# Row numbers of a group's tokens made in pairs, and other orders of scatters and loads, in a convolution with a routed MoE

## The chip, the cores and the metric

One core of one Trainium2 chip runs the kernel. The metric is the device time of one execution in microseconds (us); less is better.

## The reference

A causal convolution of 7 taps over 8 sequences of 2880 tokens with 192 channels; its taps are the softmax of a given tensor, one set per token and head (8 heads of 24 channels). Each convolved token then goes to the best of 4 groups, and in it to the best of 4 experts, and through that expert's two layers (192 to 1024, relu, 1024 to 192). The output row is scaled by both softmax values.

```python
w = softmax(weight_gen)                           # 8 x 2880 x 8 heads x 7
x = einsum('bshk,bskhg->bshg', w, x_unfolded)     # 23040 tokens x 192
g = argmax(x @ w_group); e = argmax(x @ w_expert[g])
h = relu(x @ w1[g, e]);  y = h @ w2[g, e]
out[token] = softmax(group logits)[g] * softmax(expert logits)[e] * y
```

## The kernel before

The 23040 tokens are 180 columns of 128. They are taken in 16 groups: group 0 has 12 columns, group 1 has 6, groups 2 to 14 have 12 each, group 15 has 6. For each group the kernel does three things. The convolution (`conv`) is some 26 products and sums on DVE (L318, L338), 1152 elements per partition each. `route` computes logits on TensorE, picks group and expert, and works out for every token the number of its row in a DRAM buffer, `rows`, that is sorted by expert; these numbers are the tile `pos`, and L559 turns the group's whole tile into integers, `posi`. `scatters` then sends the group's tokens there: one indirect DMA per column of 128 tokens (L593, in `scatter_row`), issued on POOL. `table` (L618 to L674) works out which blocks of `rows` a round may take.

The experts' work goes in 14 rounds. Round 1 follows group 3, round r from 2 to 12 follows group r + 2, round 13 follows group 15. A round of 2 to 12 has six blocks of 256 rows of one expert each, round 13 has 13 of these and 7 of 128 rows. For a block, SP loads its rows (`xb`, L865) and the expert's weights (L882 to L889) by table entries; ACT copies part of the rows (`xd`, L948), TensorE transposes them, ACT and DVE split them in two parts (`xh`, `xlo`; DVE rounds the weights at L920 too). Then come four units of a first matmul into `ph` (L988, ten instructions), a relu on ACT (L994), and a second matmul into `py` (L1015, eight instructions). At the end of a block ACT scales each 128 rows (L1024), and POOL sends them out by an indirect DMA (L1032): two outs per block.

Each engine runs its own instructions in the order in which the program writes them. That order comes out of a planner in the kernel: `front` is a generator that writes the convolution, routing and scatters step by step, and the block loop lets it go on until clocks modelled for each engine have caught up (`fill`, `run`). A `yield` of a number is a point on the modelled clock, `NEXT` a wait for the next unit. Scatters of a group that is not routed in a hurry wait in the list `spread`, and `front` moves its first entry on once per convolution step; groups 4 to 7 yield after every second scatter, later groups after each (L578 to L585). In the kernel before only the writing is spread: the twelve scatters of a group all wait for the one `posi`. What blocks need from SP is asked for in a list (`ask`), and `pump` issues the entries; `ask_x` asks for the rows of the next block. `load_group` loads the next group's x and taps at given convolution steps (L755).

Of the kernel before, what the change touches and what calls it, by code (L numbers as in the profile page):

```python
# [8 lines left out]
F32 = mybir.dt.float32  # L9
F32R = mybir.dt.float32r  # L10
BF16 = mybir.dt.bfloat16
I32 = mybir.dt.int32
# [22 lines left out]
def conv_moe_kernel(ctx: ExitStack, tc: tile.TileContext, x, wgen, w_group, w_expert, w1, w2, out):  # L35
# [164 lines left out]
    new_raw = [ring(f"raw{i}", m, [P, n]) for i, (n, m) in enumerate(((F, 2), (F, 2), (NFT * D, 1)))]  # L200

    grp = {}
    state = {"slots": False, "open": False, "unit": 0, "starve": False, "ph": 0, "junk": None, "urgent": False}

    def ph_tile(k, shape):
        return ps_h.tile(shape, F32, name=f"ph{k}")
# [9 lines left out]
    def run(eng, cost, *deps):  # L216
        clk[eng] = max([clk[eng]] + [d + HOP for d in deps]) + cost
        return clk[eng]
# [22 lines left out]
    def round_of(g):  # L241
        return next(r for r in range(NR) if g < ENDS[r])
# [151 lines left out]
    def route(g, o):  # L394
# [157 lines left out]
        yield 0.4  # L552
        nc.vector.tensor_tensor(out=rk, in0=rk, in1=ohf, op=ALU.mult)
        yield 0.3
        ps = rt.tile([P, SG], F32, name="pos")[:, 0:n]
        nc.vector.tensor_reduce(out=ps.unsqueeze(2), in_=rk, axis=AX.X, op=ALU.add)
        yield 0.3
        pi = rt.tile([P, SG], I32, name="posi", bufs=2)[:, 0:n]
        nc.vector.scalar_tensor_tensor(out=pi, in0=ps, scalar=-1.0, in1=ps, op0=ALU.mult, op1=ALU.max)  # L559
        yield TINY  # L560
        rest = scatters(g, xrow, pi)
        if g < MAIN:
            while spread:
                for c in spread.pop(0)[0]:
                    pass
        if 0 < g < MAIN or g + 1 == ENDS[-1]:
            for i, c in enumerate(rest):
                if g >= MAIN and i % 3 == 2:
                    yield c
            if g + 1 in ENDS:  # L570
                yield from table(round_of(g))
            state["urgent"] = False
            return
# [1 line left out]
            yield from table(round_of(g), False)  # L575
        spread.append([rest, None])

    def scatters(g, xrow, pi):  # L578
        for s in range(SIZES[g]):
            run("pool", 1.28, clk["dve"])  # L580
            scatter_row(pi[:, s:s + 1], xrow[s // SC][:, s % SC, :], round_of(g))
            if not 4 <= g < 8 or s % 2:
                yield NEXT
        if g >= MAIN and g + 1 in ENDS[:-1]:
            arrive_all(round_of(g))  # L585

# [156 lines left out]
    def front():  # L743
        side, routes = [], []
        load_group(0)
        set_up()
        load_group(1)
        yield from softmax0()
        lows.append([remainders(), 0.0])
        lower_part()  # L750
        for g in range(ENDS[-1]):
            o = grp[g]
            routes.append([route(g, o), None])
            state["urgent"] = g == FIRST
            loads = [] if g in (0, ENDS[-1] - 1) else [(0 if g < FIRST + 2 else 2, 0), (8, 1)]  # L755
            ahead = 12 if g > FIRST else 4

            def soft():
                if not o.ahead and g + 1 < ENDS[-1]:
                    o.ahead = True  # L760
                    side.append([softmax(g + 1), None])

            for n, c in enumerate(conv(g, o)):
                yield c
                if loads and n >= loads[0][0]:
                    load_group(g + 1, loads.pop(0)[1])
                if n >= ahead:
                    soft()
                for q in list(soft0):
                    yield from move(soft0, q, 1)  # L770
                if not state["urgent"]:
                    for q in side[:1]:
                        yield from move(side, q, 3)
                for q in spread[:1]:
                    yield from move(spread, q, 1)
                if routes:
                    yield from move(routes, routes[0], HURRY if FIRST <= g < MAIN else 3 if g < FIRST else 8 if g in ENDS else 2)
            while loads:
                load_group(g + 1, loads.pop(0)[1])
            soft()  # L780
            yield from finish_all(side)
            yield from finish_all(routes, 1)
            yield from finish_all(spread, 1)
        yield from finish_all(spread)
        yield from finish_all(routes)

    def finish_all(qs, keep=0):
        while len(qs) > keep:
# [59 lines left out]
    def load(n, part):  # L848
        r, nb, q = order[n]
        tab = tabs[r, nb]  # L850
        if n not in visits:
            o = visits[n] = Slot()
            o.wa = None
            if not plain(n):
                i = sum(not plain(m) for m in range(n))
                o.raw = [f(i) for f in new_raw]
            o.whole = whole(n)
            o.wc, o.ev = [], None
            o.tw, o.tlo = 0.0, 0.0
        o = visits[n]  # L860
        if part == 0:
            o.xb = xbs[n % len(xbs)][:, 0:nb, :]
            o.tx = arrive[r, nb]
            rv = nc.sync.value_load(tab[q:q + 1, 0:1], min_val=0, max_val=NROW)
            ld = nc.sync.dma_start(  # L865
                out=o.xb.rearrange("p t c -> p (t c)"),
                in_=rows[bass.ds(rv, nb * UB), :].rearrange("(p t) c -> p (t c)", t=nb))
            for m in range(r + 1, NR):
                tc.declare_no_dep(ld.ins, group=f"disp{m}", reason="a later round writes later rows")
            tc.add_to_no_dep_group(f"load{r}", ld.ins)  # L870
            return
        if not plain(n):
            while lows:
                clk["pe"] = max(clk["pe"], lows[0][1])
                lower_part()
        if o.ev is None:
            o.ev = nc.sync.value_load(tab[q:q + 1, 1:2], min_val=0, max_val=NE - 1)
        if plain(n) and part < 3:
            c = slice((part - 1) * DC, part * DC)
            nc.sync.dma_start(out=new_wa(o, F32)[0:DC, part - 1, :], in_=w1v[bass.ds(o.ev, 1), c, :].rearrange("o p f -> p (o f)"))  # L880
        elif part == 1:
            nc.sync.dma_start(out=o.raw[0], in_=w1v[bass.ds(o.ev, 1), 0:P, :].rearrange("o p f -> p (o f)"))  # L882
        elif part == 2:
            for h, src in enumerate((w1v[bass.ds(o.ev, 1), P:D, :], w1lo[bass.ds(o.ev, 1), :, :])):
                nc.sync.dma_start(out=o.raw[1][h * HP:(h + 1) * HP, :], in_=src.rearrange("o p f -> p (o f)"))
        else:
            if o.whole:
                o.wc = [wp.tile([P, NFT, D], F32, name="wc", bufs=4)]
            nc.sync.dma_start(  # L889
                out=o.wc[0] if o.whole else o.raw[2].rearrange("p (f d) -> p f d", d=D),  # L890
                in_=w2v[bass.ds(o.ev, 1), :, :].rearrange("o (f p) d -> p (o f) d", p=P))
# [165 lines left out]
    def blocks(n0, n1, paced):  # L1057
        want, jobs = [], []

        def pump(upto=None):  # L1060
            for a in list(want):
# [2 lines left out]
                if upto is not None and a[0] <= upto:  # L1064
                    need(a[0])
                if not ready(a[0]) or a not in want:
                    if upto is None:
                        break
                    continue
                want.remove(a)  # L1070
                load(*a)
# [7 lines left out]

        def ask_x(n):  # L1080
            ask(n + 1, 0)
            if n < n1 and (whole(n) or n == n0 or whole(n - 1)):
                ask(n, 3)

# [152 lines left out]
```

## Time and profile before

| | |
|---|---|
| median of the runs shown | 1311.89 us |
| runs shown | 1311.4, 1311.89, 4088.56 us |
| the profiled execution | 1310.11 us |
| its span, first to last instruction | 1308.5 us |
| mean granted TensorE clock in it | 0.963 of full |
| TensorE busy | 1187.0 us, 91% |
| DVE, ACT, POOL busy | 922.6, 662.8, 439.2 us |

The profile is of one execution; the time outside its span is 1.6 us. A busy share is a mean over stages: from the start to some 55 us the first groups are prepared, to about 1016 us convolution, routing and scatters go beside the experts' blocks, and behind 1056 us only blocks are left. An engine counts as busy while an instruction executes; issuing a DMA counts on POOL, the transfer does not.

### The profile page before, as it was taken

Reading aid. Unit: us, or ns where it says so; the run is one execution under the profiler, and the core shown is the slowest. Engines: PE = TensorE matmul, PEld = TensorE weight load, DVE = VectorE, ACT = ScalarE, POOL = GpSimd, SP = SyncE. Lnnn points to the kernel's source line nnn. Section 1 sums busy time; section 2 is a strip of 40 time slices with the busy share of each in tenths; the row PEclk is TensorE's granted clock in tenths of the full one; section 3 lists DMA queues with packets and bytes.
Section 4 is the critical chain, followed back from the end, with each engine's and each line's share of the span. In section 5 each row is a group of like instructions: output and inputs, shape, how many; then the busy total and the mean of one; then the engine's idle time right before and its main releaser. Section 6 shows DMA issues by size and latency. Waiting matters only on the chain.

```text
span 1308.5 us, 25776 instructions
## 1 busy us (share of the span) xinstructions
PE 1187.0 (91%) x9047; PEld 1142.8 (87%) x9047; DVE 922.6 (71%) x1608; ACT 662.8 (51%) x1253; POOL 439.2 (34%) x411
## 2 busy tenths in 40 slices
PE   5988889899897989898989799898899899999995
PEld 5678889889797979797989799898799899999995
DVE  7867779879687878788878698787412667767600
ACT  2523236455464545454545365454445567777631
POOL 3142251433435252525252525342421622121121
PEclk9989989999899999998999899998989999999998
DMA  8584699569677777757677676676666777777681
GB/s 255 191 262 152 194 312 319 170 230 265 209 231 239 218 229 237 241 174 240 210 217 247 182 248 206 219 211 188 181 199 181 219 229 228 228 232 214 199 253 53
DMA packets 180795, 284.96 MB, mean 218 GB/s; under 512 B 16055, under 2 KB 140823, under 8 KB 180528
## 3 DMA queue, kind: packets, MB, share of 16 engines
q1 hardware_dynamic: 160072, 239.53, 61.2%
q0 software_dynamic: 19184, 39.22, 9.0%
q10 hardware_dynamic: 1400, 4.47, 1.2%
q8 instruction: 73, 1.20, 0.4%
q14 instruction: 66, 0.54, 0.1%
HBM read 239.81 MB, written 44.23 MB: 217 GB/s over the span
## 4 chain that ended last, share of the span: by engine, by line
PE 67%; issue 20%; another core or an unknown queue 4%; POOL 3%; ACT 3%; DVE 1%; DMA 1%; POOLq 1%; ACTq 0%; DVEq 0%
PE py L1015 27%; PE ph L988 26%; POOL out L1032 3%; PE pl L409 2%; PE tp L437 1%; PE tpx L965 1%; PE py L359 1%; PE ph L359 1%; PE tpx L964 1%; PE tpx L359 1%; PE py L229 1%; PE ph L709 1%; PE tp L438 1%; PE tp L418 1%
## 5 line engine op out<-in xcount | busy, mean ns | idle before, releaser
L988 PE MATMUL ph<-xh,wa 128*128 128x256 f32 x2064 | 468.2, 302 | 7.1 <-issue 6.5
L1015 PE MATMUL py<-wc,hh 128*128 128x192 f32 x2320 | 445.9, 333 | 31.6 <-issue 28.2
L1032 POOL DMA_INDIRECT out<-xb x189 | 216.0, 1143 | 688.9 <-ACT xb L1024 475.3
L1015 PEld LDWEIGHTS py<-wc,hh 128*128 128x128 f32 x2320 | 381.9, 195 | 36.4 <-issue 32.5
L988 PEld LDWEIGHTS ph<-xh,wa 128*128 128x128 f32 x2064 | 356.9, 194 | 13.8 <-issue 11.5
L988 PE MATMUL ph<-xlo,wa 128*128 128x256 f32 x1376 | 363.5, 285 | 3.2 <-issue 3.0
L994 ACT ACTIVATE hh<-ph 128x512 f32<-128x512 f32 (+1 forms) x324 | 178.9, 553 | 369.6 <-PE ph L988 281.5
L988 PEld LDWEIGHTS ph<-xlo,wa 128*128 128x128 f32 x1376 | 265.9, 193 | 4.7 <-issue 4.2
L318 DVE TENSOR_TENSOR pr<-xin,wt 128x1152 f32<-128x1152 f32 x187 | 250.6, 1350 | 21.1 <-PE tpx L359 12.8
L593 POOL DMA_INDIRECT rows<-xrow,posi x180 | 204.3, 1135 | 158.9 <-DVE posi L559 69.3
L338 DVE TENSOR_TENSOR xrow<-xrow,pr 128x1152 f32<-128x1152 f32 x138 | 186.6, 1352 | 0.7
L920 DVE TENSOR_TENSOR wa<-raw,wa 128x1024 fp32r<-128x1024 f32 x86 | 104.9, 1220 | 92.3 <-ACT wa L902 84.9
L920 DVE TENSOR_TENSOR xlo<-tpx,xh 128x512 fp32r<-128x512 f32 x86 | 59.1, 687 | 70.4 <-ACT xh L969 52.8
L1017 PE MATMUL py<-wc,hh 128*128 128x384 f32 x352 | 107.8, 362 | 0.0
L920 DVE SCALAR_TENSOR_TENSOR hl<-ph,hh 128x512 fp32r<-128x512 f32 x88 | 60.8, 691 | 64.5 <-ACT hh L999 63.8
L1024 ACT ACTIVATE xb<-py,xb 128x192 f32<-128x192 f32 x189 | 71.9, 421 | 43.0 <-PE py L1015 20.0
L902 ACT CAST wa<-raw 128x1024 fp32r<-128x1024 f32 x86 | 90.3, 1050 | 1.1 <-DMA raw<-in_moe_w 1.1
L905 ACT CAST wa<-raw 128x1024 fp32r<-128x1024 f32 x86 | 89.7, 1042 | 0.0
L1018 PE MATMUL py<-wc,hl 128*128 128x192 f32 x352 | 88.6, 252 | 0.0
L988 PE MATMUL ph<-xd,wa 96*128 96x128 f32 x544 | 73.4, 278 | 2.5 <-ACT hh L994 1.4
L988 PEld LDWEIGHTS ph<-xd,wa 96*128 96x128 f32 x544 | 70.0, 194 | 2.6 <-ACT hh L994 1.6
L999 ACT ACTIVATE hh<-ph 128x512 fp32r<-128x512 f32 x88 | 52.6, 598 | 34.0 <-PE ph L988 26.7
(179 smaller groups left out, 1248.6 us busy)
## 6 DMA issues: line engine op xcount, KB each, us to landing
wc<-in_moe_w SPq DMA_DIRECT2D x81, 768.0 KB
raw<-in_moe_w SPq DMA_DIRECT2D x86, 512.0 KB
raw<-in_moe_w SPq DMA_DIRECT2D x96, 256.0 KB
xin<-in_x SPq DMA_DIRECT2D x26, 864.0 KB
raw<-w1lo SPq DMA_DIRECT2D x86, 256.0 KB
raw<-in_moe_w SPq DMA_DIRECT2D x22, 768.0 KB
xb<-rows SPq DMA_DIRECT2D x86, 194.0 KB
wa<-in_moe_w SPq DMA_DIRECT2D x34, 384.0 KB
```

The lines of the kernel that those rows point to most:

```text
L318: nc.vector.tensor_tensor(out=dst, in0=o.xin[:, c0 + k:c0 + k + SC, :].rearrange("p s (h g) -> p s h g", g=HG), in1=w4[:, c0:c0 + SC, :, k ...
L338: nc.vector.tensor_tensor(out=acc, in0=acc, in1=prs[k - 2], op=ALU.add)
L593: written_once(nc.gpsimd.indirect_dma_start(out=rows[:, :], out_offset=bass.IndirectOffsetOnAxis(ap=idx, axis=0), in_=src, in_offset=None, ...
L902: nc.scalar.copy(out=o.wa[:, 0, :], in_=o.raw[0])
L905: nc.scalar.copy(out=o.wa[:, 2, :], in_=o.raw[1])
L920: f(*a, **k)
L988: nc.tensor.matmul(ph[:, v, :], lhsT=w[:, f0:f0 + P], rhs=rhs, start=i == 0, stop=i == len(terms) - 1)
L994: nc.scalar.activation(out=hh, in_=ph, func=AF.Relu)
L1015: nc.tensor.matmul(b.py[t][:, 0:D], lhsT=hh[:, v, c], rhs=wc[0][:, f, :], start=f == 0, stop=f == NFT - 1)
L1017: nc.tensor.matmul(b.py[t], lhsT=hh[:, v, c], rhs=wc[f // 4][:, f % 4].rearrange("p l d -> p (l d)"), start=f == 0, stop=False)
L1018: nc.tensor.matmul(b.py[t][:, 0:D], lhsT=hl[:, v, c], rhs=wc[f // 4][:, f % 4, 0, :], start=False, stop=f == NFT - 1)
L1032: ins = nc.gpsimd.indirect_dma_start(out=out[:, :], out_offset=bass.IndirectOffsetOnAxis(ap=b.x.bitcast(I32)[:, t, D + 1:D + 2], axis=0), ...
```

## The change

Five things change.

- For groups from 4 on the conversion goes from `route` into `scatters` and is done two columns at a time, into a ring of four small tiles `pair`; the conversion stands just before the two scatters that read it. `pos` gets two buffers.
- The scatters of such a group are not begun before a block load of the round before its own has been written (`state["loaded"]`).
- The next group's loads of x and taps move from convolution steps 2 and 8 to 6 and 13 for groups from 4 on, its softmax from step 12 to 17.
- The last group waits with its own scatters until those of group 14 are written, its routing goes on beside them, and its scatters and table yield while the loads are behind.
- `ask_x` asks for the rows of the two blocks behind the next one too, in rounds from 2 on, and `pump` passes over entries that are not ready where it stopped at the first.

```diff
@@ -200,7 +200,7 @@
     new_raw = [ring(f"raw{i}", m, [P, n]) for i, (n, m) in enumerate(((F, 2), (F, 2), (NFT * D, 1)))]
 
     grp = {}
-    state = {"slots": False, "open": False, "unit": 0, "starve": False, "ph": 0, "junk": None, "urgent": False}
+    state = {"slots": False, "open": False, "unit": 0, "starve": False, "ph": 0, "junk": None, "urgent": False, "loaded": 0}
 
     def ph_tile(k, shape):
         return ps_h.tile(shape, F32, name=f"ph{k}")
@@ -552,20 +552,19 @@
         yield 0.4
         nc.vector.tensor_tensor(out=rk, in0=rk, in1=ohf, op=ALU.mult)
         yield 0.3
-        ps = rt.tile([P, SG], F32, name="pos")[:, 0:n]
+        ps = rt.tile([P, SG], F32, name="pos", bufs=2)[:, 0:n]
         nc.vector.tensor_reduce(out=ps.unsqueeze(2), in_=rk, axis=AX.X, op=ALU.add)
         yield 0.3
-        pi = rt.tile([P, SG], I32, name="posi", bufs=2)[:, 0:n]
-        nc.vector.scalar_tensor_tensor(out=pi, in0=ps, scalar=-1.0, in1=ps, op0=ALU.mult, op1=ALU.max)
-        yield TINY
-        rest = scatters(g, xrow, pi)
+        rest = scatters(g, xrow, ps)
+        while spread and g + 1 == ENDS[-1]:
+            yield NEXT
         if g < MAIN:
             while spread:
                 for c in spread.pop(0)[0]:
                     pass
         if 0 < g < MAIN or g + 1 == ENDS[-1]:
             for i, c in enumerate(rest):
-                if g >= MAIN and i % 3 == 2:
+                if g >= MAIN and (i % 3 == 2 or state["loaded"] < NR - 2):
                     yield c
             if g + 1 in ENDS:
                 yield from table(round_of(g))
@@ -575,12 +574,24 @@
             yield from table(round_of(g), False)
         spread.append([rest, None])
 
-    def scatters(g, xrow, pi):
-        for s in range(SIZES[g]):
-            run("pool", 1.28, clk["dve"])
-            scatter_row(pi[:, s:s + 1], xrow[s // SC][:, s % SC, :], round_of(g))
-            if not 4 <= g < 8 or s % 2:
-                yield NEXT
+    def scatters(g, xrow, ps):
+        n = SIZES[g]
+        step = n if g < MAIN else 2
+        while g >= MAIN and state["loaded"] < round_of(g) - 1:
+            yield NEXT
+        for s0 in range(0, n, step):
+            if g < MAIN:
+                pi = rt.tile([P, SG], I32, name="posi", bufs=2)[:, 0:n]
+            else:
+                pi = rt.tile([P, 2], I32, name="pair", bufs=4)
+            part = ps[:, s0:s0 + step]
+            nc.vector.scalar_tensor_tensor(out=pi, in0=part, scalar=-1.0, in1=part, op0=ALU.mult, op1=ALU.max)
+            run("dve", TINY)
+            for s in range(s0, s0 + step):
+                run("pool", 1.28, clk["dve"])
+                scatter_row(pi[:, s - s0:s - s0 + 1], xrow[s // SC][:, s % SC, :], round_of(g))
+                if not 4 <= g < 8 or s % 2:
+                    yield NEXT
         if g >= MAIN and g + 1 in ENDS[:-1]:
             arrive_all(round_of(g))
 
@@ -752,8 +763,8 @@
             o = grp[g]
             routes.append([route(g, o), None])
             state["urgent"] = g == FIRST
-            loads = [] if g in (0, ENDS[-1] - 1) else [(0 if g < FIRST + 2 else 2, 0), (8, 1)]
-            ahead = 12 if g > FIRST else 4
+            loads = [] if g in (0, ENDS[-1] - 1) else [(0, 0), (8, 1)] if g < MAIN else [(6, 0), (13, 1)]
+            ahead = 4 if g <= FIRST else 12 if g < MAIN else 17
 
             def soft():
                 if not o.ahead and g + 1 < ENDS[-1]:
@@ -781,8 +792,13 @@
             yield from finish_all(side)
             yield from finish_all(routes, 1)
             yield from finish_all(spread, 1)
-        yield from finish_all(spread)
-        yield from finish_all(routes)
+        while routes:
+            for q in spread[:1]:
+                yield from move(spread, q, 1)
+            q = routes[0]
+            yield from move(routes, q, 4)
+            if routes and q[1] is not None:
+                yield Until(q[1][1]) if q[1][0] == "time" else NEXT
 
     def finish_all(qs, keep=0):
         while len(qs) > keep:
@@ -868,6 +884,7 @@
             for m in range(r + 1, NR):
                 tc.declare_no_dep(ld.ins, group=f"disp{m}", reason="a later round writes later rows")
             tc.add_to_no_dep_group(f"load{r}", ld.ins)
+            state["loaded"] = r
             return
         if not plain(n):
             while lows:
@@ -1064,8 +1081,6 @@
                 if upto is not None and a[0] <= upto:
                     need(a[0])
                 if not ready(a[0]) or a not in want:
-                    if upto is None:
-                        break
                     continue
                 want.remove(a)
                 load(*a)
@@ -1079,6 +1094,9 @@
 
         def ask_x(n):
             ask(n + 1, 0)
+            for m in (n + 2, n + 3):
+                if m < n1 and order[m][0] > 1:
+                    ask(m, 0)
             if n < n1 and (whole(n) or n == n0 or whole(n - 1)):
                 ask(n, 3)
 
```

The order of POOL's instructions around the scatters of group 8, before (`rows` from `posi` is a scatter, `out` an out; x12 means twelve in a row):

```order
L1032 DMA out<-xb_135 23040x192 x2
L1032 DMA out<-xb_136 23040x192 x2
L1032 DMA out<-xb_137 23040x192 x2
L593 DMA rows<-xrow,posi 188928x194 x12
L1032 DMA out<-xb_138 23040x192 x2
L1032 DMA out<-xb_139 23040x192 x2
L1032 DMA out<-xb_140 23040x192 x2
L1032 DMA out<-xb_141 23040x192 x2
L1032 DMA out<-xb_142 23040x192 x2
```

and with the change:

```order
L1049 DMA out<-xb_137 23040x192 x2
L604 DMA rows<-xrow,pair 188928x194 x2
L1049 DMA out<-xb_138 23040x192 x2
L604 DMA rows<-xrow,pair 188928x194 x4
L1049 DMA out<-xb_139 23040x192 x2
L604 DMA rows<-xrow,pair 188928x194 x4
L1049 DMA out<-xb_140 23040x192 x2
L604 DMA rows<-xrow,pair 188928x194 x2
L1049 DMA out<-xb_141 23040x192 x2
L1049 DMA out<-xb_142 23040x192 x2
```

Where twelve scatters stood in one run, two, four, four and two now stand with the outs of three blocks between them.

The order of DVE in the same place, before (L318 and L338 are the convolution, L920 the weight rounding and the x split, L553 to L559 the end of the routing, L618 on the table):

```order
L553 TENSOR_TENSOR sel<-sel,oh 128x192
L556 TENSOR_REDUCE pos<-sel 128x12
L559 SCALAR_TENSOR_TENSOR posi<-pos 128x12
L618 TENSOR_TENSOR units<-cnt,per_unit 128x16
L619 TENSOR_TENSOR units<-units,origin_129 128x16
L620 SCALAR_TENSOR_TENSOR units<-units,done 128x16
L338 TENSOR_TENSOR xrow<-xrow,pr 128x6x192
L628 TENSOR_SCALAR n_6731<-units 128x16
```

and with the change, from the first pair of group 8 on (L588 is the conversion, L937 was L920):

```order
L588 SCALAR_TENSOR_TENSOR pair<-pos 128x2
L338 TENSOR_TENSOR xrow<-xrow,pr 128x6x192
L937 TENSOR_TENSOR wa<-raw_147,wa 128x1024
L937 TENSOR_TENSOR xlo<-tpx,xh_145 128x512
L318 TENSOR_TENSOR pr<-xin,wt 128x1152
L588 SCALAR_TENSOR_TENSOR pair<-pos 128x2
L338 TENSOR_TENSOR xrow<-xrow,pr 128x6x192
L318 TENSOR_TENSOR pr<-xin,wt 128x1152
L338 TENSOR_TENSOR xrow<-xrow,pr 128x6x192 x2
L588 SCALAR_TENSOR_TENSOR pair<-pos 128x2
```

The one conversion of twelve columns stood before the table; now each of two columns stands between instructions of the convolution, here the first three of six.

The order of DVE in group 4 with the change, from its second pair on:

```order
L588 SCALAR_TENSOR_TENSOR pair<-pos 128x2
L338 TENSOR_TENSOR xrow<-xrow,pr 128x6x192
L588 SCALAR_TENSOR_TENSOR pair<-pos 128x2
L318 TENSOR_TENSOR pr<-xin,wt 128x1152
L588 SCALAR_TENSOR_TENSOR pair<-pos 128x2
L338 TENSOR_TENSOR xrow<-xrow,pr 128x6x192 x2
L588 SCALAR_TENSOR_TENSOR pair<-pos 128x2
L318 TENSOR_TENSOR xrow<-xin,wt 128x6x192
```

Here the pairs of groups 4 to 7 stand one or two convolution instructions apart.

## Rows read from the trace of the kernel before

**Rows 1.** The page: the span, and part 1, busy time of the engines.
```profile
span 1308.5 us, 25776 instructions
...
PE 1187.0 (91%) x9047; PEld 1142.8 (87%) x9047; DVE 922.6 (71%) x1608; ACT 662.8 (51%) x1253; POOL 439.2 (34%) x411
```

**Rows 2.** Windows, all engines: stretch, length, busy (x instructions), PEclk, DMA share, GB/s.
```profile
246.00:1005.00 759.00, 691.51 (x5217) 669.66 (x5216) 565.12 (x959) 388.66 (x723) 291.91 (x250) 0.96 0.71 216
275.00:325.00 50.00, 50.00 (x405) 49.29 (x404) 47.30 (x86) 30.56 (x56) 15.96 (x12) 1.00 0.78 232
1016.00:1056.00 40.00, 33.40 (x235) 32.93 (x234) 23.08 (x64) 21.64 (x38) 22.03 (x28) 0.94 0.76 238
1060.00:1240.00 180.00, 180.00 (x1401) 180.00 (x1400) 127.52 (x184) 129.34 (x218) 34.99 (x36) 1.00 0.76 221
```

**Rows 3.** Windows of the relus L994 alone, columns as in rows 2.
```profile
246.00:272.00 26.00, 3.59 (x6) 0.87 0.56 182
272.00:298.00 26.00, 5.37 (x9) 1.00 0.67 213
935.00:961.00 26.00, 3.36 (x6) 0.80 0.61 176
961.00:987.00 26.00, 5.73 (x11) 1.00 0.69 209
246.00:1005.00 759.00, 140.36 (x235) 0.96 0.71 216
```

**Rows 4.** Windows of the scatters L593 alone.
```profile
246.00:272.00 26.00, 12.42 (x12) 0.87 0.56 182
272.00:298.00 26.00, 0.00 (x0) 1.00 0.67 213
```

**Rows 5.** Lines of L559 and L318: duration ns min/median/max, first and last start us.
```profile
L559 DVE SCALAR_TENSOR_TENSOR posi<-pos x16: 158/171/174, 56.3 to 1016.4; 128x12 int32<-128x12 f32 x14, 128x6 int32<-128x6 f32 x2
...
L318 DVE TENSOR_TENSOR pr<-xin,wt x187: 1293/1351/1372, 11.3 to 910.4; 128x1152 f32<-128x1152 f32 x187
```

**Rows 6.** Timeline of POOL: start us, busy us, engine, line, operation, [idle before <-releaser].
```profile
250.07 0.97 POOL L593 DMA_INDIRECT rows<-xrow,posi  x1 [0.30 <-DVE own L664]
251.34 0.97 POOL L593 DMA_INDIRECT rows<-xrow,posi  x1 [0.30 <-issue]
...
264.78 1.07 POOL L593 DMA_INDIRECT rows<-xrow,posi  x1 [0.30 <-issue]
266.16 0.97 POOL L1032 DMA_INDIRECT out<-xb  x1 [0.30 <-issue]
```

**Rows 7.** Timeline of TensorE in the same burst.
```profile
257.13 0.28 PE L988 MATMUL ph<-xlo,wa 128*128 128x256 f32 x1
260.55 1.01 PE L1015 MATMUL py<-wc,hh 128*128 128x192 f32 x2 [3.14 <-issue]
...
270.97 0.44 PE L437 MATMUL tp<-ident,xrow 128*128 128x128 f32 x2 [2.88 <-ACT hl L447]
```

**Rows 8.** Timeline of ACT in the same burst.
```profile
260.07 0.42 ACT L1024 ACTIVATE xb<-py,xb 128x192 f32<-128x192 f32 x1 [2.27 <-remote]
...
269.65 0.60 ACT L994 ACTIVATE hh<-ph 128x512 f32<-128x512 f32 x1 [6.37 <-issue]
```

**Rows 9.** Timeline of POOL in the stretch without scatters.
```profile
1146.49 0.97 POOL L1032 DMA_INDIRECT out<-xb  x1 [7.53 <-DVE xb L1030]
1147.77 0.97 POOL L1032 DMA_INDIRECT out<-xb  x1 [0.30 <-issue]
1156.27 0.97 POOL L1032 DMA_INDIRECT out<-xb  x1 [7.53 <-DVE xb L1030]
```

**Rows 10.** Timelines: block loads of rounds 2 and 10, and last scatter before round 10.
```profile
273.59 1.54 SPq L865 DMA_DIRECT2D xb<-rows  x2
...
820.40 1.07 POOL L593 DMA_INDIRECT rows<-xrow,posi  x1 [0.30 <-issue]
...
869.12 0.34 SPq L865 DMA_DIRECT2D xb<-rows  x1
```

## The prediction

> **What bounds the kernel now.** I read the page first: the span is 1308.5 us and TensorE is busy for 1187.0 of it, DVE for 922.6, POOL for 439.2 [rows 1]. So the end moves only as far as TensorE gains, and what it can gain is its 121 us of idle time plus the time at a lower clock. Next come the windows by stage [rows 2]. From 1060 to 1240 us, where the convolution is over, TensorE is busy for 180.00 of 180 us at clock 1.00: nothing to win. From 275 to 325 us it is busy for 50.00 of 50 although DVE is busy for 47.30: a nearly full DVE does not slow it. But over 246 to 1005 us, with groups 4 to 14 being convolved, routed and scattered, it is busy for 691.51 of 759: 67.5 us idle.
>
> Where in that stretch? The L994 relus count finished units of the first matmul. I cut eleven windows of 26 us from the start of each burst of scatters, and eleven of 26 us right behind them; the first pair and the last stand in [rows 3]. The eleven burst windows hold 6, 6, 7, 7 (groups 4 to 7) and 7, 7, 7, 6, 7, 7, 6 relus (groups 8 to 14), 73 in all; the eleven behind them hold 9, 9, 9, 10 and 9, 8, 9, 9, 9, 9, 11, in all 101. A calm window thus makes a unit in 286 / 101 = 2.83 us. The first burst window holds 12 scatters, the one behind it none [rows 4]. Cost of the bursts: 28 units, 28 x 2.83 = 79 us: groups 4 to 7 have 11 units (31 us), groups 8 to 14 have 17 (48 us). The whole stretch gives the same size: 759 - 235 x 2.83 = 94 us; and the bare idle time, 67.5, is the smallest reading of it.
>
> What happens in a burst? One L559 instruction of 0.17 us makes all 12 row numbers [rows 5], so POOL, which waits for nothing else, issues twelve scatters of 0.97 us with gaps of 0.30, one every 1.28 us, plus the outs before and behind [rows 6]. On TensorE the last matmul of a unit is recorded at 257.13, the next at 260.55 after 3.14 us idle put to "issue", and another gap of 2.88 follows [rows 7]. On ACT the L1024 that needs the product waited 2.27 us for a "remote" release, and the relu starts at 269.65, twelve microseconds after its matmul's record, again put to "issue" [rows 8]. The granted clock is 0.87 in the first burst window and 0.80 in the last, so part of each ran at the lower level (1.2 of 2.4 GHz); in the calm ones behind them it is 1.00 [rows 3]. So while POOL issues scatters back to back, completions reach the other engines late, and the idle TensorE is then granted a lower clock. Two DMAs in a row do not do this: from 1060 to 1240 us 36 outs go in pairs, 1.28 us apart and some 8.5 us between pairs [rows 9], and TensorE has no idle time there [rows 2].
>
> **The change, part by part.**
> Conversions. For groups 4 to 15 twelve L559 instructions go and 69 two-column ones come, 57 more on DVE at 0.17 us [rows 5]: 9.7 us. DVE's 565 of 759 us leaves it room [rows 2], and the calm stretch shows TensorE full beside DVE at 95%: cost taken as 0; with no cover at all it would be the 9.7 us.
>
> Scatters of groups 8 to 14. The pair instructions stand between convolution instructions of 1.35 us [rows 5], 4 to 9 us of DVE work apart, and POOL's order becomes 2, 4, 4, 2 scatters with a block's two outs between. A run of 14 to 16 becomes runs of 2 to 6, mostly separate pairs. No row shows runs of 4 to 6; pairs cost nothing (36 outs, [rows 9]), runs of 14 lose 17 units in 7 bursts, 6.9 us each. Bounds of the gain: 0 to 48. I take four fifths, since the new runs are nearer to the pair: 38 us.
>
> Scatters of groups 4 to 7. Their pairs lie only 1.5 to 5 us of DVE work apart and a pair takes POOL 2.56 us [rows 6], so with the outs between POOL stays nearly full for as long as before; the order even keeps runs of 8. Bounds 0 to 31; I take a third: 10 us.
>
> The last group. It is routed beside the scatters of group 14. In 1016 to 1056 us TensorE is idle for 6.6 us [rows 2] and the clock is 0.94. Bounds -3 to 9; I take 3.
>
> Loads asked for sooner, group loads moved to steps 6 and 13, softmax at 17. On SP the moves change which transfer waits behind which; DMA engines are busy for 0.71 of the stretch [rows 2]. In round 2 the first block load goes out 8.8 us after the last scatter's start, in round 10 48.7 us after [rows 6, 10]: it is not the scatter that the load waits for in most rounds. Bounds -10 to 10; I take 0.
>
> Rows arriving later. In group 8 the last pair lies 17 convolution steps of 1.35 us [rows 5] and six steps of rounding and splitting behind the first, 23 to 31 us, I take 29; the burst took 15 [rows 6]: 14 us later. The 48.7 us of round 10 take that; in round 2, with 8.8, the pairs are close together (some 14 us) and end no later than the burst. Cost 0, upper bound in the fourth rival.
>
> New waits. A pair instruction may wait for a place in its ring of four, with convolution, weight rounding and x splitting behind it on DVE. POOL in turn may hold a scatter behind an out that waits for its block, up to 7.53 us [rows 9]; four pairs lie further apart than that. Taken as 0, at most 7.5 us once per group, 80 in all, and that only if TensorE had no blocks ready.
>
> Sum: 38 + 10 + 3 = 51 us off the profiled execution, 1310.1: 1259. The median of the runs shown, 1311.9, is 1.8 us above that execution; so 1261.
>
> **A rule that speaks against it.** The bursts and the late completions stand in [rows 3, 6 to 8]. The Trainium skill, "SBUF — State Buffer", section "Who interferes with whom", says that a DMA never contends with a compute engine and that PE and ACT wait on no one. By it, spacing the scatters frees no TensorE time and the time stays near 1312. The windows speak against it, though they do not show what path the delay takes: [rows 3] has 28 units fewer in the burst windows. It is the second rival, with a small chance.
>
> **Rivals.**
> 1. Full recovery: groups 4 to 7 too run at the calm pace, since any gap lets late completions through. For it: 94 us by the whole stretch; against it: POOL stays busy there. 79 + 3 = 82 off: 1230. Between it and my sum lies 1245.
> 2. Nothing is recovered, because the loss goes per scatter and not per run, or because what slows the burst windows is the routing work that falls in them (L618 to L674 with the logits): 1312, with the extra DVE work unhidden 1322. Against it: 36 outs without loss, and the gaps lie under the scatters, after 257 us.
> 3. Not spread enough: POOL works in order behind outs that wait for ACT, so pairs gather and are issued in runs of 6 to 8; half of groups 8 to 14, nothing of 4 to 7: 24 off, 1288.
> 4. Slower: rows come too late. A round's last pair is held back (the planner lets no scatter start before the round before has loaded a block, and its pairs then take 29 us). Since block loads are also asked for sooner, they may stand on SP's in-order queue before their rows are there, with weight and x loads behind them. If all 14 us by which the last pair is later go onto that queue in every round, 11 x 14 = 154 us are lost, 51 gained: 1415. It decides from 7.0 us per round ((26 + 51) / 11) on. Against it: the 48.7 us of round 10, and that the planner issues a load only when its own clock has the rows there.
>
> **How the numbers follow.** My forecast 0.45 (1245 to 1277), full recovery 0.20, not spread enough 0.16, nothing recovered 0.13, slower 0.06. The likeliest gives 1261. The range 1220 to 1308 leaves out the slower case, most of the unhidden part of the second rival and the best of the first. About 2% can be told from no change: 1285.7 and 1338.1. Faster: 0.45 + 0.20 + not quite two thirds of 0.16 = 0.75; slower: 0.05 (the last case beyond 1338); same: 0.20.
>
> **What would show each step.** Right: in the changed kernel no run of L593's successor longer than 4 to 6 for groups 8 to 14, TensorE gaps of 2 us and more gone there, some 9 relus in each 26 us window, the granted clock near 1.00; groups 4 to 7 still with gaps under POOL runs. PE's busy time would fall only by its slow-clock part, the span by the idle time. Wrong: relus per window still at 6 to 7 with scatters in pairs (second rival); idle time of L948 and of TensorE put to rows loads, SP standing at a block load (fourth); DVE idle at the pair instruction (ring of four); or windows of groups 4 to 7 at the calm pace (first).

## The result and the profile after

The changed kernel took 1254.53 us in the median of four runs (1244.89 to 1258.67), the kernel before 1311.64 in the same comparison; the ratio is 0.9599, with a 95% interval of 0.9557 to 0.964. The ratio is taken over the fast runs and is not that of the two medians (0.956); one run of the kernel before took 4088.56 us. The forecast was 1261: the median is 6.5 us below it, and by the ratio, 0.9599 of 1311.64, the time is 1259.0. So the size came out nearly as worked out. The sum behind it did not, as the experiments show.

From the page of the changed kernel: the span and part 1.

```profile
span 1243.0 us, 25865 instructions
...
PE 1162.5 (94%) x9047; PEld 1122.1 (90%) x9047; DVE 923.5 (74%) x1665; ACT 660.7 (53%) x1253; POOL 443.1 (36%) x411
```

Against [rows 1]: the span is 65.5 us shorter in the profiled executions (the one after is the fastest of its four), TensorE's busy time 24.5 us shorter with the same 9047 instructions, so 41 us of the gain are idle time. DVE's 922.6 us are 923.5 now: by their own lines the 69 conversions of two columns take 10.5 us and the twelve that they replace took 2.0, but DVE's busy time as a whole grew by 0.9.

Windows of all engines, columns as in [rows 2], for the stretch from the first pair of group 4 to 1005 us and for one with blocks alone:

```profile
262.00:1005.00 743.00, 717.24 (x5573) 699.58 (x5572) 595.34 (x1084) 420.46 (x783) 321.61 (x281) 0.99 0.80 238
1020.00:1175.00 155.00, 155.00 (x1214) 155.00 (x1214) 109.71 (x159) 111.97 (x189) 31.10 (x32) 1.00 0.75 221
```

Where TensorE lacked 67.5 us of 759 in [rows 2], 25.8 of 743 are left, and the clock is 0.99. The stretch without scatters is full, as before.

The relus (L1011 was L994) in two of eleven pairs of windows, cut as for [rows 3] from each group's first scatter (groups 4 and 9), and the scatters in the second pair:

```profile
262.00:288.00 26.00, 3.60 (x6) 0.87 0.53 151
288.00:314.00 26.00, 4.24 (x8) 0.96 0.79 235
592.00:618.00 26.00, 5.43 (x9) 1.00 1.06 310
618.00:644.00 26.00, 5.39 (x9) 1.00 0.66 209
```

```profile
592.00:618.00 26.00, 7.72 (x7) 1.00 1.06 310
618.00:644.00 26.00, 5.94 (x6) 1.00 0.66 209
```

The eleven windows from the first scatter hold 6, 8, 8, 8 relus in groups 4 to 7 (26 before) and 9, 9, 10, 9, 9, 9, 9 in groups 8 to 14, 64 where it was 47. The ones behind them hold 8 to 10 (8 to 11 before). In group 9 the twelve scatters are spread over both windows: seven begin in the first, the last of them runs over the border and is counted in both, and five begin in the second. In [rows 4], of group 4 before, all twelve stood in the first. The clock is 1.00 in both windows.

In groups 4 to 7 the runs are hardly broken: ten of group 4's scatters stand, with two outs between, in one run of twelve DMAs, and group 6 still has its twelve scatters in one run of 16 DMAs from 402.2 us. The relus of group 6's first window went from 7 to 8 all the same.

POOL in group 9, and the conversion (duration ns min/median/max; who waited for it, us in all and times):

```profile
595.72 1.81 POOL L604 DMA_INDIRECT rows<-xrow,pair  x1 [0.30 <-DVE pair L588]
597.83 0.97 POOL L604 DMA_INDIRECT rows<-xrow,pair  x1 [0.30 <-issue]
602.70 1.93 POOL L1049 DMA_INDIRECT out<-xb  x1 [3.90 <-ACT xb L1041]
604.94 0.97 POOL L1049 DMA_INDIRECT out<-xb  x1 [0.30 <-ACT hh L1011]
606.22 1.08 POOL L604 DMA_INDIRECT rows<-xrow,pair  x1 [0.30 <-issue]
...
610.22 0.97 POOL L604 DMA_INDIRECT rows<-xrow,pair  x1 [0.30 <-issue]
614.50 0.97 POOL L1049 DMA_INDIRECT out<-xb  x1 [3.31 <-ACT xb L1041]
```

```profile
L588 DVE SCALAR_TENSOR_TENSOR pair<-pos x69: 96/152/159, 261.6 to 957.7; 128x2 int32<-128x2 f32 x69
...
  POOL rows L604: 33.0, 12
```

Two scatters, then two outs with four scatters, and so on: what the order of the instructions said. From group 8 on no run is longer than six DMAs. The pitch within a run is some 1.28 us, as in [rows 6].

Group 4 shows the other side. POOL's last scatter, SP's first block load of round 2, ACT and TensorE:

```profile
289.05 0.97 POOL L604 DMA_INDIRECT rows<-xrow,pair  x1 [0.31 <-issue]
...
268.58 0.01 SPq L906 DMA_DIRECT2D wc<-in_moe_w  x1
291.44 0.33 SPq L881 DMA_DIRECT2D xb<-rows  x1
...
310.33 1.04 ACT L919 CAST wa<-raw 128x1024 fp32r<-128x1024 f32 x1 [5.17 <-DMA raw<-in_moe_w]
...
312.85 0.69 PE L1032 MATMUL py<-wc,hh 128*128 128x192 f32 x1 [3.29 <-ACT xb L1041]
```

The last pair stands behind two outs and its second scatter starts 27 us after the group's first, at 262.04 us; in the burst that took 15 [rows 6]. The block load follows at 291.44 (273.59 in [rows 10]), and SP issues nothing between 268.59 and it. Weight loads stand behind it on SP, the first at 298.18: ACT waits 5.17 us for weights at 310.33, and TensorE, for what ACT does after them, 3.29.

### The profile page after: what moved, and what is told of

Its sections match the earlier page's. It is cut to its first block, busy times and chain, and to the rows that moved or that the text cites. A ratio compares the mean times of both kernels' runs of the same rounds, so it can differ in the third digit from the quotient of the medians.

```text
span 1243.0 us, 25865 instructions
## 1 busy us (share of the span) xinstructions
PE 1162.5 (94%) x9047; PEld 1122.1 (90%) x9047; DVE 923.5 (74%) x1665; ACT 660.7 (53%) x1253; POOL 443.1 (36%) x411
## 4 chain that ended last, share of the span: by engine, by line
PE 63%; issue 22%; POOL 5%; DMA 4%; ACT 2%; SPq 1%; POOLq 1%; another core or an unknown queue 1%; DVE 0%; ACTq 0%; DVEq 0%
PE py L1032 26%; PE ph L1005 25%; POOL out L1049 4%; PE pl L409 2%; PE ph L359 1%; PE py L229 1%; PE tpx L359 1%; PE py L359 1%; PE tp L437 1%; PE tpx L982 1%; POOL rows L604 1%; PE tpx L981 1%; PE ph L720 1%; DMA xb<-rows 1%; DMA raw<-in_moe_w 1%
## 5 line engine op out<-in xcount | busy, mean ns | idle before, releaser
L1005 PE MATMUL ph<-xh,wa 128*128 128x256 f32 x2064 | 457.9, 298 | 0.5 <-issue 0.5
L1032 PE MATMUL py<-wc,hh 128*128 128x192 f32 x2320 | 436.9, 329 | 16.5 <-issue 8.1
L1049 POOL DMA_INDIRECT out<-xb x189 | 221.9, 1174 | 607.7 <-ACT xb L1041 409.6
L1032 PEld LDWEIGHTS py<-wc,hh 128*128 128x128 f32 x2320 | 375.0, 192 | 19.0 <-issue 9.7
L1005 PE MATMUL ph<-xlo,wa 128*128 128x256 f32 x1376 | 356.8, 282 | 0.0
L1005 PEld LDWEIGHTS ph<-xh,wa 128*128 128x128 f32 x2064 | 349.7, 190 | 5.4 <-issue 3.9
L1011 ACT ACTIVATE hh<-ph 128x512 f32<-128x512 f32 (+1 forms) x324 | 179.0, 553 | 321.0 <-PE ph L1005 275.8
L318 DVE TENSOR_TENSOR pr<-xin,wt 128x1152 f32<-128x1152 f32 x187 | 250.8, 1351 | 19.9 <-remote 10.6
L1005 PEld LDWEIGHTS ph<-xlo,wa 128*128 128x128 f32 x1376 | 260.6, 189 | 0.7 <-issue 0.7
L338 DVE TENSOR_TENSOR xrow<-xrow,pr 128x1152 f32<-128x1152 f32 x138 | 186.6, 1352 | 0.5
L604 POOL DMA_INDIRECT rows<-xrow,pair x138 | 156.4, 1133 | 74.7 <-issue 38.9
L937 DVE TENSOR_TENSOR wa<-raw,wa 128x1024 fp32r<-128x1024 f32 x86 | 104.8, 1219 | 49.7 <-ACT wa L919 35.8
L937 DVE SCALAR_TENSOR_TENSOR hl<-ph,hh 128x512 fp32r<-128x512 f32 x88 | 60.9, 692 | 60.5 <-ACT hh L1016 59.8
L937 DVE TENSOR_TENSOR xlo<-tpx,xh 128x512 fp32r<-128x512 f32 x86 | 59.1, 688 | 46.1 <-ACT xh L986 45.8
L604 POOL DMA_INDIRECT rows<-xrow,posi x42 | 45.9, 1092 | 94.2 <-ACT hl L365 45.5
L1005 PE MATMUL ph<-xd,wa 96*128 96x128 f32 x544 | 74.0, 280 | 4.1 <-ACT hh L1011 2.3
L1005 PEld LDWEIGHTS ph<-xd,wa 96*128 96x128 f32 x544 | 70.5, 196 | 5.3 <-ACT hh L1011 2.9
```

The costliest lines, as they stand in the source:

```text
L318: nc.vector.tensor_tensor(out=dst, in0=o.xin[:, c0 + k:c0 + k + SC, :].rearrange("p s (h g) -> p s h g", g=HG), in1=w4[:, c0:c0 + SC, :, k ...
L338: nc.vector.tensor_tensor(out=acc, in0=acc, in1=prs[k - 2], op=ALU.add)
L604: written_once(nc.gpsimd.indirect_dma_start(out=rows[:, :], out_offset=bass.IndirectOffsetOnAxis(ap=idx, axis=0), in_=src, in_offset=None, ...
L937: f(*a, **k)
L1005: nc.tensor.matmul(ph[:, v, :], lhsT=w[:, f0:f0 + P], rhs=rhs, start=i == 0, stop=i == len(terms) - 1)
L1011: nc.scalar.activation(out=hh, in_=ph, func=AF.Relu)
```

## The experiments

The experiments ran in four groups, and their runs fall into two sorts. In the comparison above and in the second group the kernel before took 1311.6 us; in the first, third and fourth group it took 1200.1, 1197.8 and 1199.9. I call the two sorts place A and place B; these are names only. The record gives the first and the second group the same chip number, 13, the third 0 and the fourth 7, so the number does not tell A from B, and what does is not recorded. Only runs of one place are compared, except where one kernel is set against itself. The diffs below go from the changed kernel to the run and show its main lines; three dots stand for lines left out.

**No pairs, all else as changed.** The pairs are undone; the hold on the scatters, the moved loads, the asking and the last group's order stay.

```diff
-        for s0 in range(0, n, step):
-            ...
+        pi = rt.tile([P, SG], I32, name="posi", bufs=2)[:, 0:n]
+        nc.vector.scalar_tensor_tensor(out=pi, in0=ps, scalar=-1.0, in1=ps, op0=ALU.mult, op1=ALU.max)
+        for s in range(SIZES[g]):
+            ...
```

> The changed kernel with one conversion of all columns again, all else as changed. If the long runs are the loss: 1293 to 1312 us, with runs of 12 scatters and more and TensorE idle under them. If the other edits bring the gain: 1250 to 1270.

This ran at place B: 1195.68 us, ratio 0.9966 (0.995 to 0.9982). And once more, at place A:

> The changed kernel with one conversion of all columns again. Where the kernel before takes some 1310 us: 1293 to 1312 if the long runs are the loss, 1245 to 1265 if the other edits bring the gain. Where it takes some 1200: 1192 to 1200, and 3 to 6 us below the changed kernel, which has the late pairs.

There: 1280.66, ratio 0.9762 (0.9699 to 0.9825), below 1 with its whole interval, though not all of it is 2% below. Neither theory had that: without any pair 31 of the 1311.65 us are gone, and in its profile the twelve scatters of each group from 4 to 14 still stand in runs of 14 to 16 DMAs.

**The changed kernel and the kernel before again**, in the same group at place A.

> The changed kernel as it is. Theory: what a long run of scatters costs differs between chips, and the four variants ran on a chip where it costs nothing. Then beside a kernel before of some 1200 us it takes 1194 to 1206; beside one of some 1310 us, 1245 to 1262. Rival: the change's gain needs all its edits together, in any place; then 0.96 of the kernel before, some 1152 where that takes 1200.

> The kernel before once more, for its profile on this chip. Theory: where it takes some 1200 us, TensorE has no gap of 2 us or more under the twelve scatters in a row of groups 4 to 14, and some 9 relus stand in each window of 26 us under them as behind them. Rival: the gaps are there and time is saved elsewhere.

The changed kernel: 1267.24, ratio 0.9637 (0.9567 to 0.9706). The one run of the kernel before: 1313.91. So at place A the edits without the pairs bring 31 us, the pairs 13 more on top. The 13 are the less certain: no run with pairs (1257.99 to 1272.43) was as slow as one without (1277.18 to 1288.2), but the changed kernel's own median moved by 13 us from the comparison above to this group.

The four profiles show where. The first matmul L988 (L998, L1005) of a run of blocks marks the same work in each kernel. The first window holds 402 of these instructions (most of rounds 0 and 1), the second the next 240 (24 units, about where round 2 begins), the third the next 2400, a fourth, of two kernels, the next 910. Columns: stretch, length, busy time and count of that line on TensorE and its weight loads, PEclk, DMA share, GB/s. The kernel before at A:

```profile
111.69:231.07 119.38, 55.32 (x402) 51.75 (x402) 0.97 0.81 243
231.07:307.95 76.88, 36.08 (x240) 31.61 (x240) 0.96 0.75 225
307.95:1077.12 769.17, 363.02 (x2400) 317.24 (x2400) 0.96 0.71 215
```

The changed kernel without pairs at A:

```profile
112.06:237.13 125.07, 55.38 (x402) 51.84 (x402) 0.96 0.79 230
237.13:305.66 68.53, 35.41 (x240) 30.73 (x240) 1.00 0.86 240
305.66:1044.99 739.33, 358.00 (x2400) 311.57 (x2400) 0.97 0.76 226
1044.99:1259.05 214.06, 123.44 (x910) 113.60 (x910) 1.00 0.77 219
```

The changed kernel at A:

```profile
110.92:248.45 137.53, 59.17 (x402) 55.42 (x402) 0.90 0.76 213
248.45:325.86 77.41, 36.71 (x240) 32.24 (x240) 0.96 0.77 211
325.86:1033.10 707.24, 353.92 (x2400) 309.60 (x2400) 0.98 0.79 236
```

The changed kernel without pairs at B:

```profile
101.81:222.96 121.15, 55.83 (x402) 52.44 (x402) 0.96 0.85 246
222.96:289.48 66.52, 35.24 (x240) 30.73 (x240) 1.00 0.90 257
289.48:956.01 666.53, 351.06 (x2400) 306.63 (x2400) 1.00 0.84 250
956.01:1170.06 214.05, 123.42 (x910) 113.60 (x910) 1.00 0.77 219
```

For the long stretch, 2400 instructions: 769.2 us before, 739.3 without pairs, 707.2 with them, and 666.5 at place B without pairs. Of the 62 us gained at A in these profiles, 30 come without breaking a run and 32 with the pairs. The middle stretch is the reverse: 76.9, 68.5 and 77.4, so the pairs cost 8.9 us there. At B, where it takes 66.5 without pairs, the seven profiles below with pairs, fours or sixes (all but the wide spread) have 71.6 to 74.7, so this cost is there too. And the first stretch, with the scatters of groups 2 and 3, which the change leaves in one run, is 18.2 us longer in the changed kernel than before (119.4, 125.1, 137.5); at B it is 121.2 without pairs. 62.0 - 0.5 - 18.2 and 2 us from the rest are the 45.4 us between the two spans (1312.3 and 1266.9).

The same kernel at two places says most about the runs. The changed kernel without pairs, group 5, at A: POOL, ACT, TensorE (start us, busy us, line, operation, [idle before <-releaser]).

```profile
314.27 0.97 POOL L597 DMA_INDIRECT rows<-xrow,posi  x1 [0.30 <-DVE z L284]
315.55 0.97 POOL L597 DMA_INDIRECT rows<-xrow,posi  x1 [0.31 <-issue]
...
328.32 0.97 POOL L597 DMA_INDIRECT rows<-xrow,posi  x1 [0.31 <-issue]
...
316.44 0.60 ACT L1004 ACTIVATE hh<-ph 128x512 f32<-128x512 f32 x1 [1.88 <-PE ph L998]
...
324.37 0.60 ACT L1004 ACTIVATE hh<-ph 128x512 f32<-128x512 f32 x1 [6.10 <-remote]
327.16 0.58 ACT L979 CAST xh<-tpx 128x512 fp32r<-128x512 f32 x1 [2.19 <-remote]
331.44 0.73 ACT L1034 ACTIVATE xb<-py,xb 128x192 f32<-128x192 f32 x2 [3.70 <-remote]
...
331.92 2.61 PE L1025 MATMUL py<-wc,hh 128*128 128x192 f32 x7 [10.18 <-ACT xb L1034]
```

And at B:

```profile
297.71 0.97 POOL L597 DMA_INDIRECT rows<-xrow,posi  x1 [0.30 <-DVE z L284]
298.99 0.98 POOL L597 DMA_INDIRECT rows<-xrow,posi  x1 [0.30 <-issue]
...
311.79 0.98 POOL L597 DMA_INDIRECT rows<-xrow,posi  x1 [0.30 <-DMA raw<-in_moe_w]
...
300.25 0.60 ACT L1004 ACTIVATE hh<-ph 128x512 f32<-128x512 f32 x1 [1.88 <-PE ph L998]
...
302.73 0.60 ACT L1004 ACTIVATE hh<-ph 128x512 f32<-128x512 f32 x1 [0.63 <-PE ph L998]
...
305.66 0.60 ACT L1004 ACTIVATE hh<-ph 128x512 f32<-128x512 f32 x1
308.12 0.60 ACT L1004 ACTIVATE hh<-ph 128x512 f32<-128x512 f32 x1 [1.86 <-PE ph L998]
```

POOL issues with the same pitch, 1.28 us, in both. At B the relus of the stretch follow each other in 2.5 to 2.9 us. At A the relu due after 316.44 starts at 324.37, having waited 6.10 us for something "remote", ACT waits again for 2.19 and 3.70, and TensorE then has been idle for 10.18. In eleven windows of 26 us from the first scatter, as above, place B gives 108 relus without pairs, 9 or 10 in each. Place A gives 72 before, 82 without pairs and 92 with them. So twelve scatters in a row do not slow the other engines by themselves: at place A time is lost under them, and at B nothing of it is there.

The traces hold one more difference, in the updates of semaphores by which an engine or a DMA tells that it is done. For the same work the five traces of A hold 10,751 to 11,328 updates by DMAs, the nine of B 15,656 to 15,676, and waits put to "remote", a release near which no instruction of the program ended, stand in all five and in none of the nine. So at A the name of a releaser is weak evidence. What can be followed is the semaphore that the relu above waits for: at A TensorE ends instructions that raise it at 316.34, 318.81, 319.25, 320.23, 320.55 and 321.74, its updates are recorded at 316.35 and then at 324.29, and the relu starts at 324.37. At B, in the stretch shown, each such end has its update within 0.02 us. Slower transfers are not the reason: the packets of DMA queues q1 and q0 take 74.1% of the 16 engines' 1279.5 us at A and 79.4% of 1190.3 at B, 948 and 945 us. Why updates come late at A, and whether the recording of the trace, which loses them there, has a part in it, is not shown. Updates are missing at A in the stretch of blocks alone too, where no time is lost (214.06 and 214.05 us).

**The pairs alone**: the kernel before with the lines of the diff for `route` and `scatters`, the two buffers of `pos`, `state["loaded"]`, and the yields of the last group's scatters while loads are behind; the rest undone:

```diff
-            loads = [] if g in (0, ENDS[-1] - 1) else [(0, 0), (8, 1)] if g < MAIN else [(6, 0), (13, 1)]
-            ahead = 4 if g <= FIRST else 12 if g < MAIN else 17
+            loads = [] if g in (0, ENDS[-1] - 1) else [(0 if g < FIRST + 2 else 2, 0), (8, 1)]
+            ahead = 12 if g > FIRST else 4
...
-            for m in (n + 2, n + 3):
-                if m < n1 and order[m][0] > 1:
-                    ask(m, 0)
```

It ran three times, each time at B.

> The kernel before with the pairs alone (and the wait for a load of the round before, which the pairs need). If the long runs on POOL are the loss: nearly all of the gain, 1258 to 1272 us. If the moved loads, the earlier asking and the last group's order bring the gain: 1295 to 1312.

> The kernel before with the pairs alone, now beside a kernel before that may take some 1310 us. If the long runs are most of the loss there: 1262 to 1280, the gain of the whole change. If the pairs add only what the changed kernel is ahead of the one without them, 13 us: 1293 to 1305. Beside a kernel before of some 1200: 1195 to 1204.

> The kernel before with the pairs alone, a third time, for a chip on which the kernel before takes some 1310 us. There: 1262 to 1280 if breaking the runs by itself brings what the whole change brings, so that pairs and moved loads each relieve the same loss; 1285 to 1303 if the two add up (31 us without pairs, 13 more with them). Where the kernel before takes some 1200: 1195 to 1204 again, and the question stays open.

1199.5, 1197.51 and 1201.44 us; ratios 0.9997, 1.0003 and 1.0005, none further than 0.003 from 1 at the ends of their intervals. At place B the pairs are worth nothing. What they bring alone at place A was not measured, so neither was whether pairs and the other edits relieve the same loss.

**Fours and sixes**, four columns in a conversion and then six (`min(n, 6)`), the tile `pair` as wide:

```diff
-        step = n if g < MAIN else 2
+        step = n if g < MAIN else 4
```

> The changed kernel with four columns per conversion, so scatters go in fours. If the loss grows with a run from about its fourth DMA on: 1257 to 1272 us. If any break in a run is enough: as changed, 1245 to 1259. If it goes per scatter, whatever the run: as changed too, but then rest_alone must also be there.

> The changed kernel with six columns per conversion, two runs of six per group. If the loss grows with the length of a run: about halfway, 1272 to 1292 us. If any break is enough: as changed, 1245 to 1259. If runs have nothing to do with it: 1245 to 1259 as well, with rest_alone there too.

1199.59 and 1201.02 us, ratios 0.9994 (0.9971 to 1.0018) and 1.0003 (0.9985 to 1.0022), at place B. Where a run of twelve costs nothing these tell nothing of the length from which a run costs; that stays open.

**One edit undone at a time, one carried further**, all at place B. The first has the two lines on `loads` and `ahead` of the diff above, the second the three lines on `ask` (`pump` still passes over entries that are not ready), each in the changed kernel. The third spreads groups 4 to 7 like the later ones:

```diff
-                if not 4 <= g < 8 or s % 2:
+                if True:
```

> The changed kernel with the next group's loads and softmax at the convolution steps of before. Beside a kernel before of some 1310: 1288 to 1305 if the moved loads bring the 31 us that were there without pairs; 1258 to 1275 if the pairs make that superfluous or it lies elsewhere. Beside one of 1200: 1193 to 1206.

> The changed kernel without asking for the rows of the two blocks behind the next one. Beside a kernel before of some 1310: 1258 to 1275 if the asking is worth nothing, 1280 to 1300 if it brings most of what the kernel without pairs gained. Beside one of 1200: 1193 to 1206; below 1194 if loads asked for sooner block SP's queue in round 2.

> The changed kernel with groups 4 to 7 spread like the later ones, a pair per two units. Beside a kernel before of some 1310: 1250 to 1262 if the runs of 6 to 12 left there cost TensorE some 10 us; 1268 to 1285 if rows that then come later hold up rounds 2 to 5. Beside one of 1200: 1195 to 1204 by the first, above 1206 by the second.

Old loads: 1202.78, ratio 1.003 (1.0005 to 1.0054). No asking: 1201.26, 1.0015 (0.999 to 1.004). Neither is 2% from the kernel before, and neither says which edit brought the 31 us at A. Spread wider: 1210.75, ratio 1.0095 (1.0064 to 1.0126), slower clear of its interval. Its profile shows why. The 240 instructions of the middle stretch take 88.86 us here, 66.52 without pairs and 71.6 to 74.1 in the other four kernels of B that differ from the changed one by a single edit. All engines in it, then TensorE, POOL and SP:

```profile
221.99:310.85 88.86, 74.99 (x531) 72.72 (x530) 74.22 (x148) 40.46 (x77) 31.07 (x25) 0.88 0.74 208
```

```profile
275.10 0.48 PE L981 MATMUL tpx<-ident,xb 128*128 128x128 f32 x1 [4.29 <-DMA xb<-rows]
...
270.36 0.97 POOL L604 DMA_INDIRECT rows<-xrow,pair  x1 [0.30 <-issue]
283.46 1.49 POOL L1049 DMA_INDIRECT out<-xb  x1 [12.12 <-ACT xb L1041]
...
272.76 1.51 SPq L881 DMA_DIRECT2D xb<-rows  x2
```

The last scatter starts at 270.36, the block load at 272.76, and TensorE waits 4.29 us for the rows; POOL's next out waits 12.12 us for its block. This is the slower rival, in one round.

## Why the prediction was right, and which step was wrong

- **What bounds the kernel**: right. The end moved with TensorE's idle time and clock in the stretch of the scatters (67.5 us idle of 759, then 25.8 of 743); the stretch of blocks alone stayed full.
- **Scatters of groups 8 to 14, 38 us**: the place and the count held. I took four fifths of 17 units; all 17 came back (47 to 64). In the second take it went 45, 54, 63 (before, without pairs, with pairs): only half of it is the pairs'. Nine units at 2.83 us are 25 us, so as a term for "2, 4, 4, 2 instead of 12" the 38 is half as large again as what that take shows.
- **Scatters of groups 4 to 7, 10 us**: a third of 11 units was taken, 4 came back, in the second take 2 (27, 28, 29). The prediction had runs of 8 left there; runs of 12 and 16 DMAs were left.
- **Loads asked for sooner and moved, 0, and the last group, 3**: here the sum failed. The step was "it is not the scatter that the load waits for in most rounds. Bounds -10 to 10; I take 0." At place A the edits without the pairs took 31 us off, although the runs stayed at 14 to 16; the upper bounds of these two terms, 10 and 9, reach 19. I had put the whole loss down to the runs; that loss also goes with edits that leave the runs whole. Which of the edits does it, and by what, is open: the two kernels that take one out ran where there is no loss.
- **Rows arriving later, 0**: mis-sized. I had the pairs of group 4 end no later than the burst. They took 27 us where the burst took 15, since the last one stood behind two outs; 8.9 us of the middle stretch at A are the pairs', 5 to 8 at B. This is the fourth rival's mechanism, seen to cost time in one round, and the wider spread brings more of it. In the later rounds no loss is seen, 663.7 us with the pairs alone and 666.6 without pairs for the long stretch at B, but not because the room was left: of the rounds' first block loads the prediction shows only those of rounds 2 and 10. Before, rounds 3 to 6 had 5.0 to 20.6 us between the last scatter and that load in the two takes, rounds 7 to 12 had 35 and more. In the changed kernel it is 2.4 to 5.4 us in eight of the eleven rounds, and 3.5 in round 10, where it was 48.7. So the step "it is not the scatter that the load waits for in most rounds" does not describe the changed kernel; what the two stretches at B show is that no time is lost by it there.

```profile
829.00 1.91 POOL L604 DMA_INDIRECT rows<-xrow,pair  x1 [0.30 <-issue]
...
832.47 1.54 SPq L881 DMA_DIRECT2D xb<-rows  x2
```

- **Not in the sum**: the first stretch, 18.2 us longer in the second take, with runs the change does not touch. In the profile of the result it was 8 us longer (129.9 and 121.9). All three profiles at A with the other edits are longer there (125.1, 129.9, 137.5) than the two of the kernel before (119.4, 121.9), and at B the six kernels with those edits, two of them without one, take 120.0 to 125.7, the pairs alone 116.7 to 119.7. So a few of the 18 us may belong to the edits; the rest I count to what runs cost at A. Both are argued, not shown.
- **Conversions, new waits, 0**: right; DVE's busy time rose by 0.9 us, it never stood idle before a conversion, so the ring of four held nothing up, and POOL waited 33.0 us in all for a conversion, in 12 places.

So the time came out within a few us by luck, because errors met: in the second take at place A the long stretch gave 62 us where I had 51, nearly half of it from terms that I had taken as 0 and 3, and the first rounds gave back 18 that I had not seen. In the profiles of the result itself it was 78 and 13. The rule weighed against the change stands in the Trainium skill, "SBUF — State Buffer", "Who interferes with whom": a DMA never contends with a compute engine. The section is about the ports of SBUF. Place B agrees with what the prediction drew from it: 108 relus under the scatters, pairs worth 0. Place A, with 72 in the kernel before, does not; the waits followed there are for semaphore updates that came late, and no run here shows a wait for a port. The prediction gave the rival with this rule 0.13; for a reader of the profile at A the windows were the better guide, but nothing in that profile said that they hold for this place alone.

Of the three kernels timed at A the changed one is the fastest. At B the kernel without pairs is, by 0.3% (ratio 0.9966); the changed kernel itself was not timed there, and its nearest variants, the wide spread apart, lie between 0.9994 and 1.003.

## What to carry to other kernels

At one of two places time was lost under runs of indirect DMAs issued back to back, and a count of finished units under the runs and behind them shows how much; the count does not show why. Where it shows a loss, spread the run where the rows behind it have room, and leave it whole in the round whose first load waits for its last row. Do not give a loss to one cause because it lies under it: undo each part of a change alone, since here edits that leave the runs whole brought 31 of 44 us. And time the kernel before in every group of runs: the same kernel can stand 110 us apart, and a gain at one place can be nothing at another.

## What was not expected of the hardware

One kernel with one order of instructions took 1280.66 us in one group of runs and 1195.68 in another. POOL's pitch and the stretch of blocks alone (214.06 and 214.05 us for the same 910 matmuls of the first product) are the same, and the DMA packets take as long. Of the 89 us between the two spans 73 lie in the long stretch, where the windows under the scatters hold 82 relus at one place and 108 at the other and the ones behind them 99 and 101; 10 lie ahead of the first block, where nothing was looked at. In the run that was followed, a relu waited 6 us for an update whose matmul had ended 5.5 us before, and the traces of the slow place hold a quarter fewer updates than the others.
